# Middle words of weight folds in PSUM, an early verdict and a new instruction order in an attention and expert-layer kernel

## The chip, the cores and the metric

One core of one Trainium2 chip runs the kernel. The metric is the device time of one execution in microseconds; lower is better. A profile of one execution gives, beside it, the span from its first to its last instruction and every instruction in it.

## The reference

```python
def _attn_ref(q, k, v, a_re, a_im):        # (4, 8, 768, 48) each: B, H, S, D
    mag = np.sqrt(a_re * a_re + a_im * a_im)
    scale = np.minimum(mag, 0.999) / (mag + 1e-06)
    a_re_n, a_im_n = a_re * scale, a_im * scale
    for t in range(S):                      # complex decay, real key-value updates
        S_re, S_im = ar * S_re - ai * S_im + k_t v_t^T, ar * S_im + ai * S_re
        y[:, :, t] = einsum('bhd,bhde->bhe', q[:, :, t], S_re)

def _moe_ref(x, w_in, w_out, a, b):         # x (3072, 384), w_in (384, 2048), w_out (2048, 384)
    h = x @ w_in
    P = a[0] + a[1] * h + a[2] * h**2 + a[3] * h**3
    Q = 1.0 + abs(b[0]) * abs(h) + abs(b[1]) * h**2
    return (P / (Q + 1e-06)) @ w_out
```

The attention's output, with its heads laid side by side, is the x of the second function. The weights come as 64-bit floating-point numbers, so the kernel turns each pair of 32-bit words into one float32 itself.

## The kernel before

The sequence is cut into 6 chunks of 128 steps; a chunk of one batch is a unit, and there are 24 of them, worked on in 12 pairs. For a unit, `norm` works out decay magnitudes and angles from the loaded `AA`, `angle` and `trig` turn them into sines and cosines, `outer` scales queries and keys (`QK`) by them and writes them through DMAs into the layout `HQ`, and `attn` makes the scores, the values and the state update on TensorE and leaves the transposed output in `xT`. For each pair, `ffn` multiplies `xT` with the input weights into `ph` (512 columns, a PSUM bank, 3 in the ring), evaluates the rational function on ScalarE and VectorE (tiles `A1`, `A2`, `A3` in SBUF and `z` in a PSUM bank) into `g`, and multiplies `g` with the output weights into the two PSUM banks `po0` and `po1`. The other two of the eight banks are the ring `at` of the attention. The first two pairs run with whole float32 weights (`wi`, `wo`); the later ten with weights that `split` and `halve` have divided into two parts.

`weights` makes 28 folds: 12 of 512 columns for `w_in` and 16 of 384 for `w_out`. In a fold the raw words are loaded (`raw`, one of the rings `g`, `wh0`, `wh1`, `wh2`), ScalarE scales the high word, as a float, by 2**-112 into the result's place `st` in SBUF (line 344 in the trace), one instruction then extracts the sign or the top bits (on ScalarE at line 403, or as a zeroing on VectorE or GpSimd at line 402), and two VectorE steps put the bits together in `st` (`first`, line 407; `second`, line 411 or 413, by which engine extracted).

Every operation is an `Op` of a `Plan` that knows the engines that may run it. `plan.order` replays a recorded order, the long string `ORDER`: it fixes both the order in which instructions are given to the engines' queues and the engine of each. Where no order is recorded, a list scheduler makes one; its costs (`dve`, `act`, `pool`) and its flag `port` then say that VectorE and GpSimd exclude each other for that operation. A `Buf` of a ring with n places waits for the one n places earlier to be released.

`rouse` puts matmuls without use into the opening. DMAs are issued from SP's queue, some also from ScalarE's.

At the end a verdict is made: `values_ok` and `coefs_ok` count on VectorE whether the data lies where this way of computing is exact enough, a matmul adds the counts over the partitions, and `count` writes `bad`. Every engine loads `bad` into a register (`values_load`, line 910) and branches over `general`, a slow general version (line 911).

Of the kernel before, what the change touches and what calls it, by code (L numbers as in the profile page):

```python
# [22 lines left out]
P = 128  # L23
# [19 lines left out]
VP = 64  # L43
STAGE = ("wh0", "g", "wh1", "g", "wh2", "g")
# [171 lines left out]
def act(n, psum=False):  # L216
# [7 lines left out]
    "c-k$P37n2)7sk&s(=dyf`@tBb%vhrAV<|gP8AW4Bc9VP)iY!B9D?49bmJCG_lbx(3Su0es%aR)AMb_}#Gt6SlyyyGB^L;<Rd1pM&y`1|x*SXGhzaqgBDHSB7"  # L224
    "=-(avOB3XKZ6SxWFx<_4ppF!Thh#hANENxPadDS3o|bgY)7o+A85QNcRMSW~sqt|I8R`0roX{|-Di31|Gp0+j#!Hy|qqp?Fwv@#|PZcheIs6?JcP^u0+{ui4"
    "Qd7%GdTce{DEUy!$^$Jf{TVS?UXoX0&t$~MZS}?K6<M#(Nq3Eq!@7Yni(?~wTcxM&V9gl0rjN9k+*2p+uy2UY2zs(GSN?Pk7H;54Pv0P|&zSGDqgWj*ee`tD"
    ")WTwNM4yejnsGo?Kb3d1s$A3+vQ&FY7s+y>{WtVy-KNXsYu&`Wc$pe|KclaxdClH2`@IO+82g29pmvrOu@OE`mjoRx>?nh@ts8C^$8Pu4lOOaqU8W1%<K9zJ"
    "(!HalWU}Ye?b1c(NG0j0L*y&Y@|t|AX+cr`vwBUlwUg}AT+`8R(T%Zde4F_H4lV1JmqLA@e|qEOX?;tcbnDszt?AD5V&tZVNCPw621y#oUDeklK4@Cu66qH^"
    "&i9$NkswI`{YAtQ>lWxUc9*V<&CQrdE?y+JAv|9#mvomNFs<zdy{+#`AL(ei*mmGLfVU5HzMRs)=p=nY^2kYd{YAR!J&ksDXmcInJ|ya%wynP9_ORVzvob0="
    "Ihy4+&K-Xlr?_PJSIN6tl9|E!Z<#6|=w9=cSISv!7;Q>Oc-9(!CV5jW&|<8y*$y$|Y>2GW9wMe>rqvI1rd;<gX8&5waQ#r!f8A8h%-4!?OY`-PKUJQRx8+h)"  # L230
    "bY`}Hj$DgcXs>HkCt3#UG)ec@c1D?0YxQo$iMF(jb^F_B7*I^c#7^@Sm-oyHdmCO~@Yi!9WReb(QD8O8470oSUy`kN;o*3*z~*a~hQj+YveUmw?rRCj)OSE`"
    "wY1Y<StzA7nVj^K0*#iyoKR_M8ro^{gwxMoQ|jomM81eTpVc(U(XRTWJJb5Lw0xrdsEa&xrM2lIBkVnGD-HD%DJ3(_AV!ST#gc5oY#z@>vC|Tn346of>b#Oe"
    "?}ftXkupLHiLI=RlUeH16^`gb9S&!TyD7e*TFHIieyHQ5mb|H-Nqg3*<qq@~$^{*!vEtLpGFl$UBJeHLLGY&vY}n1IR8z^dPrsK0jg!UhAn!8I=Cj);?l5nP"
    "^M!w$8v;TlB};>tTTC8!DdglbXG^nnrM^yb?|XF_(G`3&ssyJD0iO`ii{kGBEosB0s|=MF^rm^7jCUpHHBgqax<qO-r@3|k$5k+TgQlBcDJ_rmZTputk`N+U"
    "F0X*nO4HRogqMp=O<M`g3YKV?ov#^YvrU0FU+Ns~C8x~O_Ljf8lcujTqniywn=WbxF|u0o{5PE!cz<3m6fx>$s=bE{)j@KO`rM;?WxO5%`A7N(>rMilUo>6s"
    "NDP(RSr%)KJH>mbx!S|s<K5Nu`VP9;$vx)X(v_MdzcRKj6?jaW$YbtUuc7SKmpGGOx44_U;$-cr{%X>_WcZ&?7WbREHrwp;_UjAchetbO&u4^y(ebDenMZV!"
    "N!Mii8CX}77iE|BCbsJGvJ95yGC((@*C(Z={wA+#Ye{hzd8v9-wo$tg@^8K1F7xu)x4$gcuf+N<NL~0m6s`=C8k&K+9n&w!ieHnZv3tUMq)UmXw-k4mcr#Gj"
    "nzDj@`^oR-l($wo!@}jd2F9IcMgw+qol|;J-;m0Zs7>6Vwl{Bk>pVGT+VOV~k=Arn7wCJkMK5vISLAOxM_sq7jR3Ll^-q*%KMLMaB4GRrc0WuHl}@@&X6S$9"
    "XA@z!>OtKjr~jV|tIcGjZjlA_r!UC+eBv1CUcR?l!sQ$Nl9gYz@#xeE`44gX$<Uvsx2=Ne_GO=Sa#U-wZy9RoKAg;r)XeQDYHhgD&Fn-$+UX&As7dCK-K@{b"
    "5tC?J(tUDFe|gF4%`88??vj3kN`#@YIoi$r$-51LejQFMwarcGWIKa&S+H3vePxs8uv-?hW@&Zz5AQ8$CkIgcCt&;y6ewI8!<|3L=g+cGOX|DS?PfINMX>or"  # L240
    "n!BxZqrE}@Tpo4X7E;e)MW}Tx`u&`=kSD3lO5|k<d6`e$P-X5uZ>ElsmeN7rm!@)@*czKWyHhJjJ?ejyY*k|pQibKn^L71I&*|S<O;XfxF6x!2)|qp3qD*64"
    "40Z9h&Lf&^|6G|x^;DCu&3SK<j6n(G^?7HmS!h$WJ?h?y+73q#s!@A>txG4}g%{YUPs7vVGF*n3igpeaRza?4bGZ#?Lx_8`){(WijX)3Y%&3;=QUjT;w`2%)"
    "`6{gH;4X&0A&e|1?QtpB(99ji=kJrb5&f$vr=!B@3Ekx&2*#io{fOhVsbR;MAMA0Q$m7hcOeL*n%uhO-+U)MO^9IP<+DDr4IT5_uu=jdBu3wP(s&s=SH_5)m"
# [24 lines left out]
    "5huIG=TTUE8ipNUd{v$m>K$VL->tG77^KtT<8hAHI8`nY#}u9IHpoVhhqA<wr}vAplFRS1{~wcU9B#0IQ|A^r90wl|DmheKK%WcvdBjd(d>$=m6dWQ2Cd3AQ"
    "0^jL6=$LZaLbSn={{n+#+BX"
# [4 lines left out]
def attn_moe(ctx: ExitStack, tc: tile.TileContext, qk, aa, v, w_in, w_out, coef, heads, lanes, out):  # L274
# [117 lines left out]
    def fold(n, src, st):  # L392
# [332 lines left out]
    def general(es):  # L725
# [69 lines left out]
        with tc.For_i(0, NC, 1) as c:  # L795
            for half in range(2):
# [158 lines left out]
```

## Time and profile before

| | |
|---|---|
| median of 3 runs | 631.91 us (630.39 to 634.02) |
| profiled execution, its own time | 630.88 us |
| its span | 629.2 us |
| granted TensorE clock over it | 0.993 |
| busy: TensorE, VectorE, ScalarE, GpSimd | 570.5, 563.0, 541.3, 227.1 us |

An engine's busy time is the time in which it ran an instruction; waits, register work, branches and the issuing of DMAs aren't counted. The ends of matmuls are modelled, so a wholly busy TensorE is one with work at every moment. PE is TensorE, PEld its loading of weights, DVE is VectorE, ACT ScalarE, POOL GpSimd and SP the engine that issues most DMAs. A letter q behind an engine's name means its sequencer.

### The profile page before, as it was taken

Reading aid. Unit: us, or ns where it says so; the run is one execution under the profiler, and the core shown is the slowest. Engines: PE = TensorE matmul, PEld = TensorE weight load, DVE = VectorE, ACT = ScalarE, POOL = GpSimd, SP = SyncE. Lnnn points to the kernel's source line nnn. Section 1 sums busy time; section 2 is a strip of 40 time slices with the busy share of each in tenths; the row PEclk is TensorE's granted clock in tenths of the full one; section 3 lists DMA queues with packets and bytes.
Section 4 is the critical chain, followed back from the end, with each engine's and each line's share of the span. In section 5 each row is a group of like instructions: output and inputs, shape, how many; then the busy total and the mean of one; then the engine's idle time right before and its main releaser. Section 6 shows DMA issues by size and latency. Waiting matters only on the chain.

```text
span 629.2 us, 13110 instructions
## 1 busy us (share of the span) xinstructions
PE 570.5 (91%) x5016; PEld 527.4 (84%) x5016; DVE 563.0 (89%) x982; ACT 541.3 (86%) x916; POOL 227.1 (36%) x208
## 2 busy tenths in 40 slices
PE   0038999999999999999999999999999999999994
PEld 0027776887889989999999999999999999999994
DVE  8989999999988999999998999998999987877874
ACT  7997999998999789989989799789899778587681
POOL 2001256166564642542662451433321425010030
PEclk9998999999999999999999999999999999999998
DMA  8977525561451450642433712711532614500000
GB/s 289 305 185 223 193 51 109 160 131 42 81 140 39 93 119 27 145 108 55 99 77 106 153 45 60 146 58 43 124 70 46 145 23 76 109 15 14 1 27 30
DMA packets 38806, 62.27 MB, mean 99 GB/s; under 512 B 4432, under 2 KB 25936, under 8 KB 38736
## 3 DMA queue, kind: packets, MB, share of 16 engines
q1 hardware_dynamic: 38160, 60.77, 38.7%
q10 hardware_dynamic: 576, 0.59, 0.5%
q8 instruction: 41, 0.67, 0.5%
q14 instruction: 29, 0.24, 0.1%
HBM read 37.75 MB, written 4.72 MB: 68 GB/s over the span
## 4 chain that ended last, share of the span: by engine, by line
PE 29%; ACT 28%; DVE 28%; issue 5%; DMA 5%; POOL 2%; SPq 1%; ACTq 0%; DVEq 0%; POOLq 0%
DVE A L332 12%; PE ph L637 10%; PE po L655 10%; ACT A L344 7%; ACT z L344 7%; DVE z L332 4%; PE at L576 3%; PE at L592 3%; DVE T L332 2%; DMA QK<-in_qk 2%; ACT L520 2%; PE at L607 2%; DMA g<-in_w_out 2%; DVE MM L332 2%; ACT T L520 1%
## 5 line engine op out<-in xcount | busy, mean ns | idle before, releaser
L655 PE MATMUL po<-wh,g 128*128 128x384 f32 x640 | 179.8, 341 | 1.1 <-DVE g L332 0.3
L637 PE MATMUL ph<-xT,wiH 128*128 128x256 f32 x960 | 162.1, 288 | 4.5 <-DVE A L332 3.9
L332 DVE SCALAR_TENSOR_TENSOR A<-A,co,z 128x512 f32<-128x512 f32 x176 | 130.9, 744 | 30.0 <-ACT z L344 27.3
L655 PE MATMUL po<-wo,g 128*128 128x384 f32 x428 | 145.7, 381 | 0.7 <-DVE g L332 0.7
L637 PEld LDWEIGHTS ph<-xT,wiH 128*128 128x128 f32 x960 | 135.2, 190 | 9.2 <-DVE A L332 4.6
L332 POOL TENSOR_TENSOR g<-A,g 128x512 fp32r<-128x512 f32 x49 | 67.7, 1383 | 157.0 <-ACT g L702 85.0
L637 PE MATMUL ph<-xT,wi 128*128 128x256 f32 x632 | 122.4, 312 | 0.8 <-ACT xT L338 0.8
L655 PEld LDWEIGHTS po<-wh,g 128*128 128x128 f32 x640 | 116.7, 188 | 4.2 <-issue 1.4
L637 PEld LDWEIGHTS ph<-xT,wi 128*128 128x128 f32 x632 | 99.7, 190 | 6.9 <-ACT xT L338 1.2
L344 ACT ACTIVATE z<-A,co 128x512 f32<-128x512 f32 x96 | 66.3, 690 | 38.2 <-DVE A L332 35.5
L655 PEld LDWEIGHTS po<-wo,g 128*128 128x128 f32 x428 | 79.8, 189 | 13.6 <-DVE g L332 1.4
L332 DVE SCALAR_TENSOR_TENSOR A<-A,co,ph 128x512 f32<-128x512 f32 x96 | 70.8, 740 | 3.8 <-ACT A L344 3.5
L344 ACT ACTIVATE A<-A,co 128x512 f32<-128x512 f32 x96 | 69.3, 722 | 1.8
L344 ACT ACTIVATE A<-ph,co 128x512 f32<-128x512 f32 x96 | 64.7, 679 | 5.6 <-DVE A L332 5.5
L332 DVE SCALAR_TENSOR_TENSOR z<-A,z 128x512 f32<-128x512 f32 x96 | 66.4, 691 | 2.0
L344 ACT ACTIVATE A<-ph 128x512 f32<-128x512 f32 x96 | 56.9, 592 | 7.1 <-PE ph L637 5.5
L344 ACT ACTIVATE z<-z 128x512 f32<-128x512 f32 x96 | 56.1, 584 | 2.1
L576 PE MATMUL at<-HQ 96*128 96x128 f32 x384 | 50.0, 277 | 0.5 <-ACT kT L338 0.4
L332 POOL TENSOR_TENSOR QK<-QK,RU 128x768 f32<-128x768 f32 x19 | 35.7, 1879 | 39.4 <-DMA QK<-in_qk 21.9
L576 PEld LDWEIGHTS at<-HQ 96*128 96x128 f32 x384 | 47.0, 191 | 3.4 <-ACT kT L338 1.9
L332 POOL TENSOR_TENSOR Z<-MM,Z 128x384 f32<-128x384 f32 x13 | 13.6, 1043 | 63.8 <-ACT Z L344 63.8
L332 DVE TENSOR_TENSOR ST<-at,cmask 128x512 f32<-128x512 f32 x48 | 32.2, 682 | 3.4 <-PE at L576 3.3
(176 smaller groups left out, 949.3 us busy)
## 6 DMA issues: line engine op xcount, KB each, us to landing
HQ<-Q SPq DMA_DIRECT2D x141, 128.0 KB, 5.0
AA<-in_aa SPq DMA_DIRECT2D x23, 384.0 KB, 3.3
QK<-in_qk SPq DMA_DIRECT2D x23, 384.0 KB, 4.8
V<-in_v SPq DMA_DIRECT2D x24, 256.0 KB, 5.0
g<-in_w_in SPq DMA_DIRECT2D x6, 512.0 KB, 5.5
wh<-in_w_in SPq DMA_DIRECT2D x6, 512.0 KB, 5.5
g<-in_w_out SPq DMA_DIRECT2D x8, 384.0 KB, 5.2
wh<-in_w_out SPq DMA_DIRECT2D x8, 384.0 KB, 4.8
```

The costliest lines, as they stand in the source:

```text
L332: call = lambda e: getattr(e, kind)(*map(real, args), **{k: real(x) for k, x in kw.items()})
L344: p = plan.op(dict(ACT=(act(n, psum) + more, lambda e: e.activation(o(), i(), f, **kw))), r, w)
L520: plan.op(dict(ACT=(act(2 * W), lambda e: e.activation(x(), x(), f, **kw))), (key,), (key,)).tab = 1
L576: e.matmul(pst[:, i, :], hf[:, 4 * g + i, 1, :], hf[:, 4 * g + i, 0, :], start=True, stop=True)
L592: e.matmul(py[32 * y:32 * y + 32, min(j, 2), :], l, sts[h // 4][:, h % 4, :] if q is None else hf[:, h, 0, :], start=q is None and j == 0, ...
L607: e.matmul(pd[0:96, h], kT[:, h], V[:, VP * h:VP * h + D], start=True, stop=True)
L637: e.matmul(ph[:, x * T:x * T + T].rearrange("p (h t) -> p h t", h=nb), wt[f // 4 * NJ + j][:, f % 4 * P:f % 4 * P + P], xT[:, x0:x0 + nb, ...
L655: e.matmul(po[b][:, 0:DM], gg, wt, start=(f == 0 and n == 0), stop=(f == NFF - 1 and n == len(prods) - 1))
```

## The change

In the first 21 folds the word between the steps, now called `part`, stands in a PSUM bank instead of in `st`: the rings `ph` (12 folds), `po0` (5) and `z` (4) lend their banks in turn. The scaling of the high word can run on ScalarE (as a copy with a scale, which keeps the sign; the later shift drops it) or on VectorE, and in the last 7 folds, which still use `st`, on GpSimd too. `first` then reads and writes `part` in PSUM, and `second` reads it there and writes `st`. The planner counts 61 ns more for such a step on VectorE and no exclusion of GpSimd. The copies of `halve` may run on VectorE or GpSimd as well as on ScalarE. The two outputs of the last pair are both sent from ScalarE's queue. The verdict's operations are planned ahead of the last pair's `ffn`, and the load of `bad` stands in the instruction streams ahead of TensorE's last operation but one; the branch stays at the end. The whole kernel has a new recorded order (a new string of the same kind, left out here); no function of the steady part is changed.

```diff
+STAGED = 21
+STAGE_PS = ("ph", "po0", "ph", "z", "ph")
...
         i = lambda: st.t.bitcast(U32)
+        staged = len(loads) <= STAGED
+        at = STAGE_PS[len(loads) % len(STAGE_PS)]
+        part = buf(ps, [P, 512], F32, at, PHB if at == "ph" else 1) if staged else st
+        u = lambda: part[:, 0:n].bitcast(U32)
...
-        scal(AF.Abs, n, lambda: st.t, sign, (raw,), (st,), scale=2.0 ** -112)
+        down = lambda e: e.tensor_scalar(part[:, 0:n], sign(), 2.0 ** -112, 1.0, ALU.mult, ALU.mult)
+
+        def shrink():
+            ways = dict(ACT=(act(n), lambda e: e.activation(part[:, 0:n], sign(), AF.Copy, scale=2.0 ** -112)), DVE=(dve(n, staged) + 61 * staged, down))
+            if not staged:
+                ways["POOL"] = pool(n, False), down
+            plan.op(ways, (raw,), (part,), port=not staged)
+
+        shrink()
...
         def first(e):
-            e.scalar_tensor_tensor(i(), i(), 3, low() if p.eng == "ACT" else high(), ALU.logical_shift_left, ALU.bitwise_or)
+            e.scalar_tensor_tensor(u(), u(), 3, low() if p.eng == "ACT" else high(), ALU.logical_shift_left, ALU.bitwise_or)
 
         def second(e):
             if p.eng == "ACT":
-                e.scalar_tensor_tensor(i(), high(), 1 << 31, i(), ALU.bitwise_and, ALU.bitwise_or)
+                e.scalar_tensor_tensor(i(), high(), 1 << 31, u(), ALU.bitwise_and, ALU.bitwise_or)
             else:
-                e.scalar_tensor_tensor(i(), low(), 29, i(), ALU.logical_shift_right, ALU.bitwise_or)
-
-        for f in (first, second):
-            plan.op(dict(DVE=(dve(n), f)), (raw, st), (st,), port=True)
+                e.scalar_tensor_tensor(i(), low(), 29, u(), ALU.logical_shift_right, ALU.bitwise_or)
+
+        for f, to in ((first, part), (second, st)):
+            plan.op(dict(DVE=(dve(n) + 61 * staged, f)), (raw, part), (to,), port=not staged)
...
     def halve(n, x, h, k, l):
-        scal(AF.Copy, n, h, lambda: x.t, (x,), (k,))
+        copy = lambda e: e.tensor_copy(h(), x.t)
+
+        def shrink():
+            plan.op(dict(ACT=(act(n), lambda e: e.activation(h(), x.t, AF.Copy)), DVE=(dve(n, False), copy), POOL=(pool(n, False), copy)), (x,), (k,), port=True)
+
+        shrink()
...
-            scal(AF.Abs, 512, t1, phf, (ph,), (A1,), psum=True)
+            scal(AF.Abs, 512, t1, phf, (ph, "bad") if end and k == 5 else (ph,), (A1,), psum=True)
...
-                1000 if not end else 0, eng=("SP", "ACT")[b:b + 1] if end else ("SP",))
+                1000 if not end else 0, eng=("ACT",) if end else ("SP",))
...
+        if i == NP - 1:
+            checks()
         mark = len(plan.ops)
         ffn(slice(i // 2, i // 2 + 1), 2 * (i % 2), 2, xTs.pop(i), 0, ff, ps, i < WHOLE, end=i == NP - 1)
...
-        for o in plan.order(ROUNDS):
+        steps = plan.order(ROUNDS)
+        late = [o for o in steps if o.eng == "PE"][-2]
+        for o in steps:
+            if o is late:
+                rv = nc.values_load(bad[0:1, 0:1], min_val=0, max_val=1)
             o.emit(E)
 
     fast.close()
-    rv = nc.values_load(bad[0:1, 0:1], min_val=0, max_val=1)
     with tc.If(rv > 0):
```

`checks` holds what stood at the end before: the operations of `coefs_ok`, `values_ok`, the matmul and `count`, unchanged.

## Rows read from the trace of the kernel before

**Rows 1.** Busy time by stretch: stretch and its length, then each engine's.

```profile
0.00:65.20 65.20, 21.21 (x167) 16.11 (x167) 58.31 (x133) 55.86 (x100) 6.26 (x15) 0.97 0.77 242
65.20:100.00 34.80, 34.05 (x137) 25.85 (x138) 33.95 (x62) 33.96 (x58) 15.19 (x19) 1.00 0.46 133
100.00:200.00 100.00, 100.00 (x823) 82.94 (x823) 94.26 (x166) 96.10 (x166) 57.63 (x53) 1.00 0.44 102
200.00:620.00 420.00, 413.81 (x3885) 401.53 (x3885) 374.68 (x613) 354.80 (x594) 148.03 (x122) 1.00 0.33 74
```

**Rows 2.** Timeline of TensorE from 65 us: start, us, instruction, idle before.

```profile
65.18 9.33 PE L637 MATMUL ph<-xT,wi 128*128 128x256 f32 x42 [0.79 <-ACT xT L338]
```

**Rows 3.** TensorE's waits from 65 to 630 us: total, times, longest.

```profile
PE ph L637 <- DVE A L332: 3.9, 9, 1.2
```

**Rows 4.** Chain of waits, shares by line, 10 to 38 and 37.5 to 65.2 us.

```profile
by line: DMA g<-in_w_out 25.2%; DMA wh<-in_w_out 17.5%; ACT wo L344 12.2%; ACT L520 9.2%; ACT wh L403 8.9%; ACT T L520 6.0%; ACT wi L344 5.9%; ACT g L403 5.7%; ACT wiH L344 5.6%; DVE MM L332 3.4%; ACT Q L344 3.0%; ACT CO L344 3.0%; ACT SQ L
...
by line: DVE wi L411 7.6%; issue 7.4%; DVE MM L332 7.3%; PE at L607 7.0%; PE at L592 6.9%; DVE wh L332 6.8%; DVE Q L332 6.2%; DVE SQ L332 5.8%; DVE wo L407 4.9%; ACT L520 4.6%; DVE wi L407 4.4%; DVE T L332 3.9%; DVE wo L411 3.6%; ACT CO L52
```

**Rows 5.** Busy time by stretch, line 403 on ScalarE, then line 411 on VectorE.

```profile
10.00:38.00 28.00, 6.93 (x12) 1.00 0.89 310
38.00:65.20 27.20, 4.20 (x7) 0.94 0.66 169
...
0.00:65.20 65.20, 11.55 (x18) 0.97 0.77 242
```

**Rows 6.** Groups of instructions, 0 to 65.2 us: busy us, mean ns, idle before.

```profile
L344 ACT ACTIVATE wi<-wh 128x512 f32<-128x512 f32 x5 | 3.3, 655 | 0.0
...
L407 DVE SCALAR_TENSOR_TENSOR wi<-wi,wh 128x512 uint32<-128x512 uint32 x5 | 3.4, 684 | 0.0
...
L402 POOL TENSOR_SCALAR g<-g 128x384 f32<-128x384 f32 (+1 forms) x2 | 1.4, 708 | 8.6 <-ACT wo L344 7.8 <-ACT wi L344 0.7
```

**Rows 7.** Costliest groups of the whole span, from the page.

```profile
L344 ACT ACTIVATE z<-A,co 128x512 f32<-128x512 f32 x96 | 66.3, 690 | 38.2 <-DVE A L332 35.5
...
L344 ACT ACTIVATE A<-A,co 128x512 f32<-128x512 f32 x96 | 69.3, 722 | 1.8
...
L332 DVE SCALAR_TENSOR_TENSOR z<-A,z 128x512 f32<-128x512 f32 x96 | 66.4, 691 | 2.0
```

**Rows 8.** Timeline where VectorE and GpSimd run at once, two places.

```profile
50.58 1.09 POOL L332 TENSOR_TENSOR Z<-MM,Z 128x384 f32<-128x384 f32 x1 [45.65 <-ACT Z L344]
50.73 1.50 DVE L411 SCALAR_TENSOR_TENSOR wi<-wh,wi 128x512 uint32<-128x512 uint32 x1
...
608.56 0.75 DVE L332 SCALAR_TENSOR_TENSOR A<-A,co,z 128x512 f32<-128x512 f32 x1
608.62 1.30 POOL L332 TENSOR_TENSOR g<-A,g 128x512 fp32r<-128x512 f32 x1 [1.46 <-ACT g L702]
```

**Rows 9.** Timeline of the tail, 614 to 630 us.

```profile
617.01 0.16 DVE L332 COPY ncar<-MM 128x3 f32<-128x3 f32 x1
...
620.89 0.34 PE L655 MATMUL po<-wh,g 128*128 128x384 f32 x1
621.27 0.62 DVE L332 TENSOR_SCALAR A<-po,co 128x384 f32<-128x384 f32 x1 [2.12 <-PE po L655]
...
621.80 0.17 DVE L871 TENSOR_SCALAR fl<-fl 128x24 f32<-128x24 f32 x1
621.92 0.39 ACTq L326 DMA_DIRECT2D out<-A  x1
...
623.28 0.14 DVE L895 TENSOR_SCALAR bad<-nok 1x1 int32<-1x1 f32 x1
```

**Rows 10.** Lines 910 and 911: ns min/median/max, first and last start us.

```profile
L910 PEldq TENSOR_LOAD <-bad x1: 486/486/486, 623.5 to 623.5; - x1
...
L911 PEldq COMPARE_BRANCH  x1: 3898/3898/3898, 624.1 to 624.1; - x1
...
L911 ACTq EVENT_SEMAPHORE  x1: 17/17/17, 627.0 to 627.0; - x1
```

More of the change, by code (lines that the diff above doesn't have):

```diff
@@ L228 @@
[L228 to L243, printed above, removed]
@@ L810, in general, with values_ok @@
                 run_ffn(bass.ds(c, 1), 2 * half, 2, xT, 0, gf, gq, plain=True)
+    def values_ok(e):
+        e.tensor_scalar(fl[:, 1], fl[:, 1], -W, None, ALU.add)
+        e.tensor_tensor(fl[:, 1], fl[:, 1], fl[:, 1], ALU.mult)
+        for i, most in enumerate((2000.0, 0.09, 12.0)):
+            e.tensor_scalar(fl[:, i], fl[:, i], most, None, ALU.is_le)
+        e.tensor_scalar(okn, ncar.rearrange("p b j -> p (b j)"), 2.0 ** -46, None, ALU.is_ge)
+        e.tensor_reduce(cnt[:, 0:1], fl.rearrange("p x n -> p (x n)"), AX.X, ALU.add)
+        e.tensor_reduce(cnt[:, 1:2], okn, AX.X, ALU.add)
@@ new lines, in coefs_ok @@
+    def coefs_ok(e):
+        e.tensor_tensor(cf[:, 4:5], cf[:, 0:1], cf[:, 1:2], ALU.add)
+        e.tensor_tensor(cf[:, 4:5], cf[:, 4:5], cf[:, 3:4], ALU.mult)
+        e.tensor_tensor(cf[:, 5:6], cf[:, 2:3], cf[:, 2:3], ALU.mult)
+        e.scalar_tensor_tensor(cf[:, 6:7], cf[:, 4:5], 16.0, cf[:, 5:6], ALU.mult, ALU.is_ge)
+        e.tensor_tensor(cf[:, 4:5], babs[:, 0:1], babs[:, 0:1], ALU.mult)
+        e.scalar_tensor_tensor(cf[:, 7:8], babs[:, 1:2], 16.0, cf[:, 4:5], ALU.mult, ALU.is_ge)
+        e.tensor_scalar(cf[:, 8:9], cf[:, 3:4], 2.0 ** -20, None, ALU.is_ge)
+        e.tensor_scalar(cf[:, 9:10], babs[:, 1:2], 2.0 ** -20, None, ALU.is_ge)
+        e.tensor_scalar(cf[:, 10:14], cf[:, 0:4], 2.0 ** 20, None, ALU.is_le)
+        e.tensor_scalar(cf[:, 14:16], babs, 2.0 ** 20, None, ALU.is_le)
+        e.tensor_reduce(cnt[:, 2:3], cf[:, 6:16], AX.X, ALU.add)
@@ new lines, in count, with checks @@
+    def count(e, pc):
+        e.tensor_reduce(nok[0:1], pc[0:1, 0:3], AX.X, ALU.add)
+        e.tensor_scalar(bad[0:1], nok[0:1], P * (3.0 * NC * B + B * NJ + 10.0) - 0.5, None, ALU.is_le)
+    def checks():
+        scal(AF.Abs, 4, lambda: cf[:, 0:4], lambda: av, ("ab",), ("cf",))
+        plan.op(dict(DVE=(1460, coefs_ok)), ("ab", "cf"), ("cf", ("cnt", 1)), port=True)
+        plan.op(dict(DVE=(700, values_ok)), (*(("fl", i, n) for i in range(2) for n in range(NC * B)), *(("fl", 2, n) for n in range(0, NC * B, 2)),
+                                            *(("ncar", b) for b in range(B))), (("cnt", 0), "fl"), port=True)
+        pc = buf(ps, [P, 512], F32, "at", 2)
+        pe(60, lambda e: e.matmul(pc[0:1, 0:3], ones, cnt, start=True, stop=True), (("cnt", 0), ("cnt", 1)), (pc,))
+        plan.op(dict(DVE=(300, lambda e: count(e, pc))), (pc,), ("bad",))
@@ L868, in attn_moe @@
             plan.spread(mark, WHOLE - 0.7, WHOLE + 0.5)
-    def values_ok(e):
-        e.tensor_scalar(fl[:, 1], fl[:, 1], -W, None, ALU.add)
-        e.tensor_tensor(fl[:, 1], fl[:, 1], fl[:, 1], ALU.mult)
-        for i, most in enumerate((2000.0, 0.09, 12.0)):
-            e.tensor_scalar(fl[:, i], fl[:, i], most, None, ALU.is_le)
-        e.tensor_scalar(okn, ncar.rearrange("p b j -> p (b j)"), 2.0 ** -46, None, ALU.is_ge)
-        e.tensor_reduce(cnt[:, 0:1], fl.rearrange("p x n -> p (x n)"), AX.X, ALU.add)
-        e.tensor_reduce(cnt[:, 1:2], okn, AX.X, ALU.add)
@@ L893, in count @@
-    def count(e):
-        e.tensor_reduce(nok[0:1], pc[0:1, 0:3], AX.X, ALU.add)
-        e.tensor_scalar(bad[0:1], nok[0:1], P * (3.0 * NC * B + B * NJ + 10.0) - 0.5, None, ALU.is_le)
-    scal(AF.Abs, 4, lambda: cf[:, 0:4], lambda: av, ("ab",), ("cf",))
-    plan.op(dict(DVE=(1460, coefs_ok)), ("ab", "cf"), ("cf", ("cnt", 1)), port=True)
-    plan.op(dict(DVE=(700, values_ok)), (*(("fl", i, n) for i in range(2) for n in range(NC * B)), *(("fl", 2, n) for n in range(0, NC * B, 2)),
-                                        *(("ncar", b) for b in range(B))), (("cnt", 0), "fl"), port=True)
@@ L901, in attn_moe @@
-    pc = buf(ps, [P, 512], F32, "at", 2)
-    pe(60, lambda e: e.matmul(pc[0:1, 0:3], ones, cnt, start=True, stop=True), (("cnt", 0), ("cnt", 1)), (pc,))
-    plan.op(dict(DVE=(300, count)), (pc,), ("bad",))
     plan.close()
     with tc.manual_schedule():
-        for o in plan.order(ROUNDS):
+        steps = plan.order(ROUNDS)
[3 more added lines that the diff above has]
+                rv = nc.values_load(bad[0:1, 0:1], min_val=0, max_val=1)
```

88 lines of the change are left out of this document (46 added, 42 removed).

## The prediction

> **What bounds the kernel now.** I read the stretches first, then TensorE's waits, then the chain of waits of the opening, then the tail instruction by instruction.
>
> The stretches [rows 1] cut the span at 65.2 us, where the first FFN matmul runs [rows 2]. Ahead of the cut TensorE is busy for 21.2 of 65.2 us, while VectorE has 58.3 and ScalarE 55.9: together 114.2 of 130.4, 87.6%. GpSimd has 6.3 and the DMA engines 77%. Behind the cut TensorE sets the pace: 34.05 of 34.8, 100 of 100 and 413.8 of 420 us, so it idles for only 6.9 us there. Its longest wait in that part is for VectorE's A tiles, 3.9 us over nine times [rows 3]. So there are three places to win: the opening of 65.2 us, the 6.9 us of gaps, and the tail.
>
> In the chain of waits of 10 to 38 us [rows 4] ScalarE stands nearly alone beside two DMA waits; the folds' extraction on ScalarE (line 403) is 8.9 + 5.7 = 14.6% of it, 4.1 us. Behind it, to 65.2 us, most of the named pieces are VectorE's [rows 4]. From 10 to 65.2 us line 403 ran 12 + 7 = 19 times on ScalarE, 6.93 + 4.20 = 11.1 us [rows 5].
>
> The tail [rows 9]: the last matmul ends at 620.89 + 0.34 = 621.23. VectorE evacuates to 621.89 and then counts the verdict, from 621.80 to 623.42, with nothing beside it. Each engine loads the verdict (0.49 us on TensorE's sequencer) and branches; TensorE's branch takes 3.90 us, from 624.1 to 628.0, and the span ends at 629.2 [rows 10].
>
> **The change, part by part.**
>
> *PSUM operands on VectorE.* 21 folds write both VectorE steps differently: 42 instructions. A 512-wide step from SBUF to SBUF takes 684 ns [rows 6]; the nearest row with one SBUF and one PSUM input and a PSUM output takes 691 ns [rows 7]. So +7 ns, 0.3 us for 42. The bounds are 0 and, by the 0.75 us of a step that reads PSUM and writes SBUF [rows 8] (it also reads a scalar from memory), +66 ns, 2.8 us; I take 0.3, because the 691 ns row has just these operands.
>
> [...]
>
> *Shrink on ScalarE.* The same form of activation from SBUF takes 722 ns into SBUF and 690 into PSUM [rows 7]: -32 ns, at most 21 x 0.032 = 0.7 us off ScalarE. On VectorE instead it costs about the 691 ns of a 512-wide PSUM step: k shrinks moved there are +0.69k us of VectorE and -0.65k of ScalarE, where a 512-wide one takes 655 ns [rows 6].
>
> *GpSimd is let in.* While GpSimd's Z ran from 50.58 to 51.67, VectorE's fold step with two SBUF inputs took 1.50 us in place of 0.69; at 608.6 a VectorE step with one PSUM input took its 0.75 us beside a GpSimd op of 1.30 that was not lengthened [rows 8]. So the staged steps, 11.55 us for 18 second ones in the opening [rows 5] and as much for as many first ones, leave some 23 us in which GpSimd can work without holding VectorE up. Moving the 19 extractions to GpSimd needs 19 x 0.708 = 13.5 us [rows 6], which fits. That takes 11.1 us from ScalarE. What does it do to the end of the opening? By the chain 4.1 us lie on the path in 10 to 38 us, but the DMA engines are 89% busy there [rows 5], so this part can shrink by no more than 11% of 28 us, 3 us; a further 4.2 us of extraction lies in 38 to 65 us, where the chain is mostly VectorE's, and I count a quarter of it, 1 us. So 4.0 us. The upper bound is by load: (114.2 - 11.1) / 2 / 0.876 = 58.8 us, 6.4 us earlier, and with 4 us of VectorE's two-input work passed to GpSimd as well (99.1 / 2 / 0.876 = 56.6), 8.6 us. The lower bound is 0: the path stays on VectorE and the transfers.
>
> An earlier first matmul is a gain only if TensorE keeps its pace behind it. It does where the folds keep up, and those left over get the same relief; I take all 4.0.
>
> *The five banks.* FFN tiles come behind the staged words in the same rings: the first `ph` waits for fold 17, the second for fold 19, the third for fold 20, `z` for fold 18, `po0` for fold 21. At the old pace 18 folds were done by 65.2 us [rows 5], and the first layer runs alone for 9.3 us from there [rows 2] before `po0` is written: 42 records in that time, twelve to a `ph` tile, make 2.7 us from one `ph` to the next. I cost it at 0 while the fold work goes no slower relative to the first FFN; its cover is this margin, a few us.
>
> *Verdict early.* The VectorE steps from 621.80 to 623.42 leave the path, as does the load, 623.5 to 624.0. They land in the last FFN, where VectorE and ScalarE wait on each other in turn (ScalarE's z activations idle 38.2 us over the kernel, 35.5 of it for VectorE [rows 7]) and TensorE is full [rows 1]; if they fell into the last chain of steps they would cost up to 1.3 us. Each engine now waits for the verdict ahead of TensorE's last but one step: behind it stand on VectorE and ScalarE only the two evacuations and the output DMAs, which wait for TensorE anyway, and on TensorE six matmuls (about 0 to 0.5 us, the load's 0.49; I take 0.25). SP and GpSimd have nothing behind it. New end: ScalarE issues the last DMA to 622.31 [rows 9], and in the old trace its next event came 2.9 us after its branch (about 624.1 to 627.0 [rows 10]); TensorE's branch takes 3.9 us from about 621.4. Both come to 625.2 or 625.3, and the old 1.2 us from 628.0 to the end give 626.5: -2.7, less the 0.25: -2.4 us. The bounds are -1.1 (1.3 us lost in the last chain) and -2.8.
>
> *Both last outputs on ScalarE's queue.* The first issue (0.39 us) has VectorE's evacuation (0.62 us) beside it [rows 9]; if it started as late as that one's middle it would hold the second up by 0.1 us. I take 0.
>
> *New order and the free choice for the splits' copies.* The rows don't show it. It can win no more than the 6.9 us of gaps. In 100 to 200 us VectorE has 94.3 and ScalarE 96.1 of 100, so it can lose as easily. I take 0, bounds -3 to +3.
>
> Sum: 630.88 (the profiled execution's own time) - 2.4 - 4.0 = 624.5. That execution is 1.0 us below the median 631.91; I put the forecast at 625.0. The difference from the median is 1.1%; what a measurement of this kernel can tell from no change is 0.5%, 3.2 us.
>
> **The rivals.**
>
> 1. *The opening gives nothing.* VectorE, 58.3 of 65.2 us, keeps all its fold steps, and if it and the transfers bind, ScalarE's relief is idle time. For it: the second half of the chain is mostly VectorE's [rows 4]. Against: 4.1 us of the first half are line 403. Time 631.9 - 2.4 = 629.5, within 0.5%.
> 2. *The load decides.* GpSimd takes extraction and part of VectorE's work, and the opening is 6.4 to 8.6 us shorter. Time 631.9 - 2.4 - 7.5 = 622.0, down to 617.9 with 8.6 and 3 us more from the gaps. For it: GpSimd stood idle for 45.65 us up to its Z [rows 8]. Against: the DMA engines at 89%.
> 3. *VectorE becomes fuller: slower.* Shrinks go to VectorE at 0.69 us each, and the 42 steps pay the 66 ns of the upper bound: 8 shrinks are 5.5 us, with 2.8 it is 8.3 us on an engine that is already 89% full, and the staged folds gate `ph`, so the first FFN waits. It decides from 5.6 us of net lateness (2.4 + 3.2). Time 631.9 - 2.4 + 8.3 = 637.8. [...] Against: the 691 ns row, and that ScalarE remains the cheaper place for a shrink.
> 4. *The early verdict isn't early.* If `bad` comes late in the new order, all five engines hold for it ahead of the last matmuls, and the tail gains nothing: 631.9 - 4 = 627.9. Against: nothing that it reads is written late except the last carry, which the old order has at 617.0 [rows 9] with nothing waiting for it.
>
> **How the numbers follow.** Forecast (opening 2 to 6 us, tail about 2.4): 0.53, own range 622 to 628.5. Rival 1: 0.17. Rival 2: 0.17. Rival 3: 0.07. Rival 4: 0.06. The range 617 to 631 holds all of rivals 2 and 4 and most of rival 1. Faster by over 0.5% means under 628.75: forecast 0.51, rival 2 0.17, rival 4 0.04, of rival 1 0.05: 0.77. Slower by over 0.5%: 0.07. The same: 0.16.
>
> **What would show it.** Right: the zeroing way of the extraction (line 402) on GpSimd some 15 times or more before the first FFN matmul, that matmul at about 61 us, VectorE's PSUM fold steps within 20 ns of 0.69, ScalarE under 50 us busy ahead of it, verdict steps before 615 us, and under 6 us from the last matmul to the end of the span, against 8.0. Wrong: the first FFN matmul still at 65 us (rival 1), waits of `ph` on fold steps or more than 15 shrinks on VectorE (rival 3), TensorE waiting for the verdict (rival 4), or gaps behind the first FFN matmul above 10 us, which would say that the new order costs what the opening wins.

## The result and the profile after

| | before | after |
|---|---|---|
| median, 18 runs each | 631.71 us (629.84 to 634.08) | 624.81 us (620.58 to 630.59) |
| ratio | | 0.9888 [0.9872, 0.9903] |
| profiled execution, its span | 630.88, 629.2 us | 625.25, 623.5 us |
| first FFN matmul | 65.18 us | 58.53 us |
| end of the last matmul | 621.23 us | 618.55 us |
| from there to the end of the span | 7.94 us | 4.99 us |

The change makes the kernel 1.1% faster: 6.9 us by the medians, where 6.9 were forecast (625.0 against 631.91). In the profiled executions the opening gives 6.65 us, the stretch from the first FFN matmul to the last matmul takes 560.02 us where it took 556.05, so 4.0 are given back, and the tail gives 2.95: 6.65 - 4.0 + 2.95 = 5.6 = 630.88 - 625.25. Forecast were 4.0, 0 and 2.4. These three terms rest on one profile of each kernel; experiment 6 and the part on the forecast say how firm they are. The line numbers have moved: the first FFN is L656, the second L674, the folds' scaling L409, the extraction L417 (ScalarE) and L416 (zeroing), the steps L421 (`first`), L425 and L427 (`second`), `halve` L440 and L443.

The stretches of after, as in [rows 1]: stretch, length, then busy time and instructions of TensorE, its weight loads, VectorE, ScalarE and GpSimd, the granted clock, the DMA share.

```profile
0.00:58.50 58.50, 19.50 (x166) 15.70 (x166) 50.67 (x108) 50.44 (x91) 27.72 (x36) 1.00 0.87 278
58.50:100.00 41.50, 39.55 (x167) 29.36 (x168) 39.02 (x67) 39.29 (x68) 21.87 (x24) 1.00 0.38 108
100.00:200.00 100.00, 96.93 (x799) 79.72 (x798) 97.38 (x167) 90.96 (x154) 49.78 (x47) 1.00 0.39 93
200.00:615.00 415.00, 410.48 (x3871) 400.12 (x3871) 377.08 (x639) 346.28 (x580) 155.82 (x123) 1.00 0.35 77
```

In the opening VectorE has 25 instructions and 7.6 us less than in [rows 1] and ScalarE 5.4 us less, while GpSimd goes from 6.3 to 27.7 us. A part of this is work put off: the 11 instructions of `coefs_ok`, 1.7 us of VectorE, and 4 of the 8 split copies that ScalarE had there now run behind the first FFN matmul (a fifth went to GpSimd). Behind the opening TensorE is no longer full: it idles for 1.95 us to 100 us, 3.07 to 200 and 4.52 to 615, 9.5 in all, where it was 6.9 (0.75, 0 and 6.2). In 100 to 200 us VectorE is busy for 97.4 of 100 (94.3 before).

What GpSimd took is seen in the groups of the opening (busy us, mean ns; compare [rows 6]):

```profile
L334 POOL TENSOR_TENSOR T<-AA,SQ 128x384 f32<-128x384 f32 x3 | 3.0, 1014 | 4.6 <-ACT SQ L346 4.6
L421 DVE SCALAR_TENSOR_TENSOR ph<-ph,wh 128x512 uint32<-128x512 uint32 x3 | 2.1, 690 | 1.7 <-ACT wh L417 1.7
L425 DVE SCALAR_TENSOR_TENSOR wi<-wh,ph 128x512 uint32<-128x512 uint32 x3 | 2.0, 677 | 0.0
L409 ACT ACTIVATE ph<-wh 128x512 f32<-128x512 f32 x3 | 1.8, 613 | 0.0
```

The extraction stayed on ScalarE, 18 times ahead of the first FFN matmul; GpSimd zeroed only twice. It took two-input products of `norm` and `outer` (`T`, `SQ`, `Z`, `RU`, `QK`, `Q`), which were VectorE's. The 512-wide steps with the word in PSUM take 677 and 690 ns, as the 684 of SBUF did; the shrink into PSUM takes 613 ns where it took 655.

The output DMAs of the tail, as in [rows 9] (the last matmul ends at 618.55):

```profile
618.74 1.27 ACTq L328 DMA_DIRECT2D out<-A  x2
```

And the branch over the general version, L938, by engine (ns, then start), as in [rows 10]:

```profile
L938 PEldq COMPARE_BRANCH  x1: 4022/4022/4022, 617.1 to 617.1; - x1
...
L938 ACTq EVENT_SEMAPHORE  x1: 17/17/17, 622.6 to 622.6; - x1
```

`bad` is written at 574.9 us. TensorE's sequencer begins its 4.0 us branch at 617.1, 1.5 us before the last matmul has ended, and is through at 621.2. The end is now ScalarE's: its two DMA issues last until 620.01, it branches, and its next event comes 2.6 us later, at 622.6.

### The profile page after: what moved, and what is told of

Its sections match the earlier page's. It is cut to its first block, busy times and chain, and to the rows that moved or that the text cites. A ratio compares the mean times of both kernels' runs of the same rounds, so it can differ in the third digit from the quotient of the medians.

```text
span 623.5 us, 13130 instructions
## 1 busy us (share of the span) xinstructions
PE 570.0 (91%) x5016; PEld 527.9 (85%) x5016; DVE 566.1 (91%) x982; ACT 527.6 (85%) x891; POOL 255.2 (41%) x229
## 5 line engine op out<-in xcount | busy, mean ns | idle before, releaser
L674 PE MATMUL po<-wh,g 128*128 128x384 f32 x640 | 180.6, 342 | 1.4 <-POOLq L938 0.7
L656 PE MATMUL ph<-xT,wiH 128*128 128x256 f32 x960 | 161.3, 288 | 0.4 <-DVE A L334 0.2
L674 PE MATMUL po<-wo,g 128*128 128x384 f32 x428 | 146.8, 383 | 1.6 <-DVE g L334 1.6
L656 PEld LDWEIGHTS ph<-xT,wiH 128*128 128x128 f32 x960 | 135.6, 192 | 3.8 <-issue 1.8
L334 POOL TENSOR_TENSOR g<-A,g 128x512 fp32r<-128x512 f32 x51 | 70.3, 1384 | 152.5 <-ACT g L721 76.7
L656 PE MATMUL ph<-xT,wi 128*128 128x256 f32 x632 | 123.1, 313 | 1.8 <-DVE A L334 1.0
L674 PEld LDWEIGHTS po<-wh,g 128*128 128x128 f32 x640 | 116.8, 188 | 4.2 <-issue 1.2
L656 PEld LDWEIGHTS ph<-xT,wi 128*128 128x128 f32 x632 | 99.9, 191 | 8.9 <-DVE A L334 2.1
L674 PEld LDWEIGHTS po<-wo,g 128*128 128x128 f32 x428 | 79.4, 189 | 14.5 <-DVE g L334 3.2
L346 ACT ACTIVATE A<-ph,co 128x512 f32<-128x512 f32 x96 | 65.2, 682 | 4.3 <-DVE A L334 3.1
L334 POOL TENSOR_TENSOR QK<-QK,RU 128x768 f32<-128x768 f32 x17 | 32.3, 1902 | 46.0 <-DVE RU L334 27.2
L334 DVE TENSOR_TENSOR_SCAN MM<-MM,ncar,SQ 128x128 f32<-128x128 f32 x69 | 36.8, 541 | 0.1
```

Of the source, the lines that this page charges most:

```text
L334: call = lambda e: getattr(e, kind)(*map(real, args), **{k: real(x) for k, x in kw.items()})
L346: p = plan.op(dict(ACT=(act(n, psum) + more, lambda e: e.activation(o(), i(), f, **kw))), r, w)
L656: e.matmul(ph[:, x * T:x * T + T].rearrange("p (h t) -> p h t", h=nb), wt[f // 4 * NJ + j][:, f % 4 * P:f % 4 * P + P], xT[:, x0:x0 + nb, ...
L674: e.matmul(po[b][:, 0:DM], gg, wt, start=(f == 0 and n == 0), stop=(f == NFF - 1 and n == len(prods) - 1))
```

## The experiments

Times are medians with their lowest and highest; ratios are to the kernel before, run on the same chip. All edits but two are to the kernel after. "Arrival" is the start of the first FFN matmul.

**1. The words back in SBUF, the new order kept.**

```diff
-STAGED = 21
+STAGED = 0
```

> The changed kernel in its own order and with its own engines, but all 28 folds keep the middle word in SBUF. Theory A (the PSUM words let GpSimd work beside the fold steps): GpSimd is busy 22.7 us behind its setup in the 58.5 us opening, so some 40% of the 36 fold steps ahead of the first FFN matmul meet a GpSimd operation and wait about 0.6 us: 9 us on VectorE; the first FFN matmul moves from 58.5 to 64 to 68 us and the time to 629 to 634 us. Theory B (the new order and its choice of engines are the gain, PSUM or not): 624 to 626 us, first FFN matmul below 60 us.

Measured: 634.91 us (633.37 to 635.92, 6 runs), ratio 1.0051 [1.0037, 1.0065]: slower than before, and 10.1 us slower than after. Arrival 68.47. One of the opening's fold steps beside GpSimd (a group of four like it has a mean of 1328 ns):

```profile
33.56 2.13 POOL L334 TENSOR_TENSOR QK<-QK,RU 128x768 f32<-128x768 f32 x1 [2.62 <-DMA QK<-in_qk]
...
33.95 2.15 DVE L425 SCALAR_TENSOR_TENSOR wo<-wh,wo 128x384 uint32<-128x384 uint32 x1
```

A step of 0.55 us takes 2.15: it ends 0.41 us behind GpSimd's product, which had begun 0.39 us before it. Eleven VectorE instructions lose 9.65 us in this way ahead of 60 us; in the kernel after, with the words in PSUM, none of these steps does (541 to 565 ns at 384 columns, 670 to 700 at 512). GpSimd waits as well, and longer. Its `MM<-SQ` here, and the same operation in the kernel after:

```profile
43.63 5.03 POOL L334 TENSOR_SCALAR MM<-SQ 128x384 f32<-128x384 f32 x1 [5.38 <-DVE SQ L334]
```

```profile
39.22 0.51 POOL L334 TENSOR_SCALAR MM<-SQ 128x384 f32<-128x384 f32 x1 [5.92 <-DVE SQ L334]
```

It takes 5.03 us in place of 0.51, while VectorE runs nine fold steps in a row to 48.30, and TensorE then waits 3.95 us for the `Q` that GpSimd makes behind it. So nearly half of the 9.9 us by which the arrival is later is GpSimd held up by VectorE, which the expectation had not counted. The step of 2.15 us shows VectorE held up by one product of GpSimd; the 5.03 us show GpSimd held up through a run of nine steps and not through one. By what the two engines hold each other up is not shown.

**2. The words in PSUM, the old order kept** (the kernel before, 21 folds fitted to the banks free in its order).

```diff
...
-        scal(AF.Abs, n, lambda: st.t, sign, (raw,), (st,), scale=2.0 ** -112)
+        scal(AF.Copy, n, lambda: part[:, 0:n], sign, (raw,), (part,), scale=2.0 ** -112)
...
-        for f in (first, second):
-            plan.op(dict(DVE=(dve(n), f)), (raw, st), (st,), port=True)
+        for f, to in ((first, part), (second, st)):
+            plan.op(dict(DVE=(dve(n), f)), (raw, part), (to,), port=True)
```

> The kernel before in its own order and with its own engines, but 21 folds keep the middle word in the five PSUM banks (other folds than in the change, so that the old order holds). Theory A: GpSimd has nothing to do in that opening, so only the scaling gets faster, by 0.05 us in each of 21: 630.5 to 632 us, first FFN matmul at 64 to 65.2 us. Theory C (a word in PSUM quickens the folds by itself): 626 to 629 us.

Measured: 631.37 us (629.59 to 632.19, 11 runs), ratio 0.9991 [0.998, 1.0001]. The banks alone give nothing that can be told from the spread. Its profiled execution has no fall of the clock in the opening (see experiments 5 and 6), and TensorE's timeline shows the arrival:

```profile
62.67 9.33 PE L643 MATMUL ph<-xT,wi 128*128 128x256 f32 x42 [0.77 <-ACT xT L340]
```

**3. GpSimd's work of the opening given to VectorE** (25 operations ahead of the first FFN matmul; the words stay in PSUM).

```diff
+                plan.ffn = getattr(plan, "ffn", plan.ops[-1])
...
+        opening = steps[:steps.index(plan.ffn)]
+        for o in opening:
+            if o.eng == "POOL" and "DVE" in o.ways:
+                o.eng = "DVE"
```

> The changed kernel with the 25 GpSimd operations ahead of the first FFN matmul given to VectorE, in the same order; the words stay in PSUM. Theory A: VectorE gets some 13 us more in an opening in which it is busy 50.7 of 58.5 us, so the first FFN matmul comes at 65 to 71 us and the time is 630 to 637 us. Rival D (ScalarE and the transfers set the opening, VectorE has room): 624 to 627 us.

Measured: 629.31 us (626.68 to 630.62, 7 runs), ratio 0.9955 [0.9939, 0.9972]: +4.5 us, between what the two theories gave. Arrival 65.11, but with the granted clock at 0.50 from 49.3 to 62.9 us.

The same kernel once more:

> The changed kernel with the opening's GpSimd work on VectorE, unchanged from its first run, for a second profile: in the first one TensorE's clock was at half from 49.3 to 62.9 us, and the first FFN matmul came at 65.1 us. Without such a drop, theory A has that matmul at 61 to 63 us; rival D (VectorE had room) at 58 to 60 us.

It took 628.56 us, with the clock at 0.50 again, from 51.7 to 61.9, and the arrival at 65.02. So the arrivals don't separate GpSimd's help from the clock. The second profile does so ahead of its fall: the first `at<-V,kT` matmul starts at 51.41 us, and at 47.82 in the kernel after. In experiment 4, which has no fall and arrives at 62.47, it starts at 51.52. That is 3.6 us for GpSimd's help. The times give about the same: its three runs with a mean granted clock of 0.995 or 0.996 took 626.68, 628.60 and 629.45 us, and the five such runs of the kernel after 623.63 to 626.07 (middle one 624.83), some 4 us less.

**4. Neither: words in SBUF and no GpSimd work in the opening** (the edits of 1 and 3 together).

```diff
+STAGED = 0
...
+        for o in opening:
+            if o.eng == "POOL" and "DVE" in o.ways:
+                o.eng = "DVE"
```

> The changed kernel in its own order, with the words in SBUF and the 25 GpSimd operations ahead of the first FFN matmul on VectorE: neither half of the pairing of PSUM words and GpSimd work. Beside the three kernels that have both, one or the other (medians 624.8, 634.9 and 629.3 us) it completes a table of four. Theory A (the PSUM words are worth something only beside GpSimd work): the same as with PSUM words and no GpSimd work, 628.5 to 630.5 us. Theory C (the PSUM words quicken the folds by themselves): 632 to 636 us. Either way what it has on the kernel before, some 2 to 3 us, is the tail's.

Measured: 627.08 us (624.02 to 629.86, 6 runs), ratio 0.9914 [0.9889, 0.994], lower than either theory gave; arrival 62.47, without a fall of the clock. The four medians together:

| | GpSimd helps | it doesn't |
|---|---|---|
| words in PSUM | 624.8 | 629.3 |
| words in SBUF | 634.9 | 627.1 |

GpSimd's help without the banks costs 7.8 us; with them it gives 4.5. The pair stands 2.3 us below doing neither (1.6 us by the two ratios, as the chips differ), and the intervals (0.9872 to 0.9903 and 0.9889 to 0.994) just overlap: that the pair is worth something beside neither is likely and not shown. Most of the change's gain is there without the banks, 632.4 - 627.1 = 5.3 us against the kernel before on the same chip: the tail, the new order and the split copies.

**5. The load of the verdict late; the first of the last outputs on SP** (two kernels, one profile of each).

```diff
-            if o is late:
-                rv = nc.values_load(bad[0:1, 0:1], min_val=0, max_val=1)
...
+    rv = nc.values_load(bad[0:1, 0:1], min_val=0, max_val=1)
     with tc.If(rv > 0):
```

> The changed kernel with only the load of the verdict back at the very end; the verdict itself stays early. Tail theory: TensorE's branch (4.0 us in the trace of the change, begun at 617.1 us, ahead of its last matmul) then begins 0.5 us behind the last matmul and sets the end: 6.0 to 6.4 us from the last matmul to the end of the span, in place of 4.99. Rival (ScalarE's output DMAs set the end either way, the load costs them 0.5 us): 5.4 to 5.6 us.

```diff
-                1000 if not end else 0, eng=("ACT",) if end else ("SP",))
+                1000 if not end else 0, eng=("SP", "ACT")[b:b + 1] if end else ("SP",))
```

> The changed kernel with the first of the last two outputs sent from SP's queue again. In the change ScalarE's queue is busy with both issues to 620.0 us, and its branch and the end follow. Theory: ScalarE then issues only the second output, from 619.3 to 619.7 us, and the tail is 0.2 to 0.4 us shorter, 4.6 to 4.8 us. Rival (SP's own way to the end is longer): 5.0 us or more.

From the last matmul's end to the span's the late load takes 5.57 us and SP's queue 5.50, against 4.99: 0.58 and 0.51 more, the rival's numbers in both. In SP's run the last event is SP's own, at 627.6 us, as the rival has it. For the late load it is less clear: ScalarE's time from its branch to its next event, which ends the kernel there, varies from 2.6 to 3.2 us between the profiles by itself. The times say less. The late load took 623.66 us, with an arrival at 58.05. SP's took 630.69, though its edit touches the last output alone, because its arrival was 63.19. The matmul with which the two part, in SP's run and then in the kernel after:

```profile
46.70 0.85 PE L584 MATMUL at<-ident,HQ 128*128 128x128 f32 x8 [3.26 <-DMA HQ<-Q]
```

```profile
44.65 0.99 PE L584 MATMUL at<-ident,HQ 128*128 128x128 f32 x8
```

In SP's run TensorE waits 3.26 us for the DMAs that write `HQ`, and the other engines have gaps behind it; its granted clock is then 0.50 from 48.5 to 55.3, and the first FFN matmul comes 4.7 us late. Of these 4.7 us 2.05 are there ahead of the fall: the delay begins with the transfers and not with the clock.

**6. The kernel before, once more**, for the size of such a fall in its own opening.

> The kernel before, unchanged, for a second profile. In the first one TensorE's granted clock fell to half from 54.3 to 57.7 us. If that drop set the first FFN matmul's start, a profile without it has that matmul at 62.5 to 63.5 us, as the kernel with PSUM words in the old order had (62.7 us, no drop). If it did not, 64.5 to 65.5 us.

It took 632.6 us; the clock was at 0.50 from 55.4 to 58.8, as from 54.3 to 57.7 in the first profile, and the arrival was 64.3. What the kernel before does without the fall is not shown by it; experiment 2's 62.67 is the nearest. It shows something else, though: from the first FFN matmul to the last this execution takes 558.6 us, where the first profile has 556.05, and its tail is 8.0 us. Against it the change's terms are 5.8, -1.4 and 3.0 us in place of 6.65, -4.0 and 2.95. So the first two terms are known from one profile each to some 2.5 us only.

**7. The verdict late** (its last three steps and the load behind everything else; `coefs_ok` stays early).

```diff
+            mark = len(plan.ops)
             checks()
+            verdict = plan.ops[mark + 2:]
...
         for o in steps:
-            if o is late:
-                rv = nc.values_load(bad[0:1, 0:1], min_val=0, max_val=1)
-            o.emit(E)
+            if o not in verdict:
+                o.emit(E)
+        for o in steps:
+            if o in verdict:
+                o.emit(E)
 
     fast.close()
+    rv = nc.values_load(bad[0:1, 0:1], min_val=0, max_val=1)
```

> The changed kernel with the verdict's last steps (the counts of the data, the matmul, the final comparison) and the load of the verdict back at the very end. Tail theory (the counts and the load stood alone on the path): 3.0 us more than the change, 627.3 to 628.5 us, and 7.5 to 8.2 us from the last matmul to the end of the span. Rival (the tail is set by the branch and the output transfer, the counts run beside them): 624.5 to 625.5 us.

Measured: 629.14 us (626.03 to 633.73, 12 runs), ratio 0.9957 [0.9932, 0.9983], 4.3 us above after, with a wide spread. In the profile the tail is 8.56 us, +3.6; arrival 57.97 and the stretch between 560.9 stay as they were. Time and tail lie a little past the tail theory's numbers and far from the rival's.

**8. The split copies.** First all on ScalarE again (11 copies that the new order has on GpSimd or VectorE):

```diff
+    halves = []
...
+        halves.append(plan.ops[-1])
...
+        for o in halves:
+            o.eng = "ACT"
```

> The changed kernel with the 11 copies of the weight split that it runs on GpSimd (10) and VectorE (1) back on ScalarE. Theory M1 (the gain is given back up to 200 us because VectorE is full there, 8 us of it held up by GpSimd): GpSimd has 6 us less in 57 to 122 us, VectorE is held up less, and the time is 622.5 to 624.5 us. Rival M2 (ScalarE's relief is what keeps TensorE going there): 5.5 us more on ScalarE, 625.5 to 628 us.

Then no low parts of the split weights: the subtractions run on 8 columns of 512 or 384, the other columns' low parts are left out, and the matmuls read the high part in their place, so that TensorE's work stays the same.

```diff
-        mul(n, lambda: l.t, lambda: x.t, lambda: h().bitcast(F32), (x, k), (l,), ALU.subtract, EN["wlo"])
+        mul(8, lambda: l[:, 0:8], lambda: x[:, 0:8], lambda: h()[:, 0:8].bitcast(F32), (x, k), (l,), ALU.subtract, EN["wlo"])
...
-            for wt, hl in ((wi, 0),) if whole else ((wiH, 0), (wiL, 0), (wiH, 1)):
+            for wt, hl in ((wi, 0),) if whole else ((wiH, 0), (wiH, 0), (wiH, 1)):
...
-                            prods = ((g[:, 0, x, t], h), (g[:, 0, x, t], woL[f].t), (g[:, 1, x, t], h))
+                            prods = ((g[:, 0, x, t], h), (g[:, 0, x, t], h), (g[:, 1, x, t], h))
```

> The changed kernel without the low parts of the split weights: their 28 subtractions cover 8 columns only, and the matmuls that read a low part read the high part, in the same number. That takes some 7 us of VectorE's and 16 us of GpSimd's work out of 60 to 250 us and leaves TensorE's and ScalarE's alone. Theory M1 (VectorE binds up to 200 us): the stretch from the first FFN matmul to the last one falls from 560.0 to 555 to 557 us, and the time to 620 to 622.5 us. Rival M3 (TensorE's new order makes its own gaps): 559 to 561 us, and 624 to 625.5 us.

The copies on ScalarE: 628.41 us (627.72 to 629.15, 6 runs), ratio 0.9937 [0.9917, 0.9958], +3.6 us, against theory M1; the arrival is 57.9, the stretch behind it 563.6 for 560.0. Without low parts: 620.93 us (618.89 to 624.95, 5 runs), ratio 0.982 [0.9788, 0.9852], -3.9 us; that stretch is 553.2 (some 1.7 us of the difference, estimated as half of 3.4 us at 0.50, is a fall of the clock at 290 us, which the profile of after has and this one not). The copies on ScalarE from 58.5 to 100 us, and then no low parts from 100 to 200:

```profile
58.50:100.00 41.50, 37.52 (x151) 27.04 (x149) 38.50 (x64) 39.07 (x67) 19.70 (x19) 1.00 0.36 105
```

```profile
100.00:200.00 100.00, 99.41 (x819) 82.03 (x817) 96.70 (x171) 93.89 (x161) 39.04 (x52) 1.00 0.40 96
```

With the copies on ScalarE TensorE is busy for 37.5 us to 100 us, where it was 39.55 in after; from 100 to 200 us it is nearly the same, 96.5 for 96.9. More on ScalarE costs time and less on VectorE and GpSimd gives it, so up to 200 us both sides bind and TensorE doesn't. Without the low parts TensorE is at 99.4 again from 100 to 200 us, where experiment 3, with the low parts and an arrival at 65.1 like this one's 64.8, has 96.7. So theory M1 alone is not enough: ScalarE counts too.

**9. More split copies on GpSimd** (14 further ones behind the first FFN matmul), as a version that might beat the change.

```diff
...
+        for o in halves:
+            if steps.index(o) > steps.index(plan.ffn):
+                o.eng = "POOL"
```

> The changed kernel with all copies of the weight split behind the first FFN matmul on GpSimd, 14 more than it has there. Theory M2 (between the first FFN matmul and 200 us ScalarE's load counts as VectorE's does; 11 copies put on ScalarE cost 3.6 us): 7.6 us less on ScalarE give 2 to 3.5 us, 621 to 623 us. Rival M1 (there VectorE alone counts, and more GpSimd work holds it up more often): 624.5 to 627 us.

Measured: 625.47 us (622.64 to 630.13, 6 runs), ratio 0.9904 [0.9875, 0.9932]. The profiled run, of 622.64 us, has a stretch of 557.3 for 560.0, the median no gain; it lies in rival M1's range. With a spread of 7.5 us this stays undecided; no version was shown to beat the change.

## Why the forecast came out, step by step

The sum was right partly by luck. By the two profiled executions two misses cancel: the opening gave 2.65 us more than was counted, the stretch behind it 4.0 less, and the tail 0.55 more. Both large misses hold a fall of TensorE's clock, for 3.4 us each: before's to 0.51 in the opening and after's to 0.50 at 290 us.

*PSUM operands: right.* +7 ns were taken, with bounds of 0 and +66. The rows show -7 and +6 ns at 512 columns [rows 6], and at 384 columns 558 where 553 to 554 were usual before. The shrink gained 42 ns, not 32.

*GpSimd let in: the place was right, the cargo wrong.* The argument that steps with one SBUF input leave GpSimd room holds for these steps (677 and 690 ns beside 27.7 us of GpSimd's work), and experiment 1 prices the other case at 10 us. But the forecast sent the 19 extractions there and so relieved ScalarE; the new order sent VectorE's two-input products and relieved VectorE most. That is half of rival 2, and the opening moved as rival 2 has it: by its formula the two engines' load, 50.67 + 50.44 = 101.1 us, gives 101.1 / 2 / 0.876 = 57.7 us, and 58.5 was measured. The chain's 3 + 1 us looked for the gain in the wrong stage. The first `Q` reaches TensorE no sooner (before, then after):

```profile
37.44 1.22 PE L619 MATMUL po<-Q,cmask 128*128 128x256 f32 x2 [13.55 <-DVE Q L332]
```

```profile
38.41 6.59 PE L638 MATMUL po<-Q,cmask 128*128 128x256 f32 x16 [18.66 <-DVE Q L334]
```

From 10 to 38 us the DMA share is 0.93 where it was 0.89, so the bound on these 28 us is not refuted; 0.87 for 0.77 over the whole opening is nearly the same transfers in less time. The gain lies behind that point, where a single us had been counted: 20.1 us from it to the first FFN matmul, 27.7 before. One part of the 6.65 us is not the change's: before's profile has its clock at 0.51 for 3.4 us. Against the 62.67 of experiment 2, without such a fall, the opening gives 4.1 us. There the 4.0 was right in size, by luck, as neither its cargo nor its stage was.

*The five banks at 0: right.* TensorE's waits from 58 to 620 us name no fold (total, times, longest):

```profile
PE at L595 <- ACT kT L340: 1.7, 1, 1.7
PE po L674 <- DVE g L334: 1.6, 3, 0.8
...
PE po L674 <- POOLq L938: 0.7, 1, 0.7
```

Ahead of the first FFN matmul 21 first and 20 second steps have run, where it was 20 and 19 (the 18 of [rows 5] are those of line 411 alone; one more stands at line 413). The third row isn't the verdict's: it is the matmul at 614.22, which reads the last `g` that GpSimd wrote.

*Verdict early: right, the terms a little off.* 2.4 us were taken, 2.95 came, and experiment 7 gives 3.6 back. The 0.25 us charged for TensorE's load were not paid, since its branch starts ahead of the last matmul's end (617.1 for 618.55), and both outputs on ScalarE, counted at 0, are worth some 0.5 (experiment 5, one profile). The load's own place is worth at most some 0.6, so most of the gain is the VectorE steps and the matmul of the count. The new end is ScalarE's second issue and branch, not TensorE's.

*New order and split copies at 0, bounds 3: mis-sized by the profiles, not refuted.* They cost 4.0 us there: 4.3 us more of idle time on TensorE to 200 us, 1.7 less behind it, and 1.4 more of busy time for the same matmuls. The last is the clock. The first of the waits above stands at 288 us: ScalarE makes that `kT` behind two loads of its function tables, of 1.28 us each. All eleven kernels with the new order have the wait (1.6 to 1.7 us), before's order has none, and in six of them, after among them, the clock falls for 3.4 us behind it (rows in the last section). The late load of experiment 5 runs the same order without that fall in 558.34 us, with 548.9 us of busy time, as before's 549.1. Against before's two profiles, 556.05 and 558.6, the new order then costs 2.3 us or nothing, which lies within the bounds.

A gain is hidden in it: the free choice of the copies gives 3.6 (experiment 8). And a part is the earlier FFN itself, which runs into a VectorE that was already at 94 of 100: with the same order and the same clock behind it, an arrival at 62.5 to 65.1 us makes the stretch 1.5 to 2.5 us shorter (experiments 3 and 4: 557.6 and 558.4 with the fall at 290 us, for after's 560.02; 556.8 without, for 558.34), though SP's run of experiment 5, late for another reason, has 560.3. "An earlier first matmul is a gain only if TensorE keeps its pace" was said, and the pace was then taken for granted. VectorE is held up there by GpSimd as well, now that split and products meet:

```profile
125.72 1.81 POOL L334 TENSOR_TENSOR Q<-QK,T 128x768 f32<-128x768 f32 x1
...
125.78 2.30 DVE L334 TENSOR_TENSOR wi<-wi,wiH 128x512 fp32r<-128x512 f32 x1
```

A low part of 0.68 us takes 2.30; the four such on VectorE to 200 us have a mean of 1087 ns, where it was 676. How much of the loss to 200 us is this and how much plain load no run tells apart.

*The signs.* Right: steps within 20 ns, the verdict before 615 us, under 6 us of tail, gaps under 10 us behind the first FFN matmul (9.5). The arrival, 58.5 for "about 61", is past the mark. Wrong: zeroing on GpSimd fifteen times, and ScalarE under 50 us (50.4). Rival 1 falls with the arrival, rival 3 with the steps (no shrink of a staged fold ran on VectorE), rival 4 with the 574.9 us of `bad`.

## What to carry to other kernels

In these runs a product on GpSimd was cheap only beside VectorE steps with one operand in PSUM: with both in SBUF each engine held the other up (a step of 0.55 us took 2.15, a GpSimd operation of 0.51 us took 5.03). Move the operand first, and price the pair together, since each half alone gave nothing or lost, and the pair itself some 2 us beside neither. When an opening is shortened, look at the engine that is second behind the bound in the next stretch; here up to 4.0 of 6.65 us were taken back. Compare openings and stretches only between profiles in which the clock did the same. A decision at the end of a kernel should be counted and loaded while the matmuls still run.

## What was not expected of the hardware

TensorE's granted clock fell to 0.50 or 0.51 in the opening of some executions: for 3.4 us in both profiles of before, 6.8 us in experiment 1 and in SP's run, 13.6 and 10.2 us in the two profiles of experiment 3, and 13.6 us without low parts, where the opening's program up to the first low part is that of after; in after and six others not at all in the opening. Before's row (the granted clock is the third number from the end):

```profile
54.30:57.70 3.40, 3.40 (x42) 2.74 (x40) 3.29 (x5) 0.76 (x3) 0.00 (x0) 0.51 1.03 383
```

Ahead of the falls TensorE had stood idle for a part of the time: in experiment 3, 6.20 of the 9.3 us to 49.3 were busy, and 5.00 of the 8.5 us to 48.5 in SP's run, against 9.06 of 9.3 and 8.26 of 8.5 in after. In SP's run, without low parts and in the first profile of experiment 3 it had waited for the DMAs of `HQ` just before, for 3.26, 3.04 and 2.86 us. The late load waits 2.08 us there (6.97 of 9.3 us busy), experiment 4 is busy for 3.58 of the 5 us from 45 to 50, and both kept a clock of 1.00, so rows don't give the condition. With the wait and the fall the arrival was 4.7 us later than in after in SP's run and 6.3 without low parts.

Behind the opening after has a fall too, from 290.0 to 293.4 us, behind the wait of 1.66 us for `kT`. The same 3.4 us in after and in the late load of experiment 5, which has the wait and not the fall:

```profile
290.00:293.40 3.40, 3.40 (x18) 3.40 (x17) 2.37 (x2) 3.34 (x6) 1.21 (x1) 0.50 0.32 58
```

```profile
290.00:293.40 3.40, 3.40 (x31) 3.40 (x30) 2.11 (x2) 3.34 (x6) 0.96 (x1) 1.00 0.32 64
```

TensorE is busy throughout in both, with 18 matmuls and 31. Of the 18 runs of after, the two with the lowest mean clock, 0.989 and 0.988, took 627.36 and 630.59 us; the other 16 have 0.995 or more and took 620.58 to 626.07.
